# Causal attention and a routed second attention on one core: last queries of two head pairs in one set of 64x64 products, all scores in float32, tiles cleared ahead, a new order

## Chip, cores and metric

The kernel runs on one core of a Trainium2 chip. The metric is the device time of one launch in microseconds (us); lower is better. Engines: TensorE (PE in the profile, PEld its weight loads), VectorE (DVE), ScalarE (ACT), GpSimd (POOL), SyncE (SP), whose queue issues all DMAs here.

## What is computed

Batch 4, 12 heads of 64, 448 positions, all float32. First layer: causal softmax attention per head. Its output x (4, 448, 768) goes into a second layer with four experts, each a causal attention with one head of 64, whose outputs are weighted by a gate that keeps the two best of four experts:

```python
scores = np.where(mask, -1e9, 0.125 * q @ k.T)
attn = np.exp(scores - scores.max(-1)); attn /= attn.sum(-1) + 1e-9
x = heads_joined(attn @ v)
logits = x @ w_gate
for e in range(4):
    y[e] = causal_attention(x @ wq[e], x @ wk[e], x @ wv[e]) @ wo[e]
out = sum of w[token, e] * y[e] over the token's two experts
```

## The kernel before

**Work items.** The heads go in pairs: 24 pairs in the first layer (4 batches of 6) and 8 in the second (4 batches of 2 expert pairs). The 448 queries of a head are three blocks of 128 and a rest of 64. For a pair, `attention` (L384) lists these steps:

- Scores (L428 to L443). The two heads sit in the two halves of the 128 partitions, so a product contracts 64 rows, and the two heads' products (64x128 tiles) go to two PSUM banks. Block i meets only its first 128(i+1) keys. Blocks are made in two groups, block 1 and blocks 0 and 2.
- The last 64 queries of both heads (L447 to L454) are made in one product with 128 rows and 128 columns: the host writes these queries twice, each time with the other head's rows zero (L789), so that 128 contracted rows give head 0 in 64 output partitions and head 1 in the other 64. All 448 keys, one bank.
- Maximum on VectorE (L411), exponential on ScalarE (L417), reciprocal (L457), normalisation on GpSimd (L348; on ScalarE too in the second layer, L346).
- The weights are turned to have keys on partitions: for the pairs in `VIA` by two VectorE transposes (L485) and four SBUF-to-SBUF DMAs (L491), otherwise by 16 TensorE transposes in four banks (L500), each copied by ScalarE or VectorE.
- pv (L527): 128x64 tiles, the two heads side by side in the columns of the array. For each head and each of the two passes it streams 256+128+64 + 256+64 + 128+64 + 64 = 1,024 columns.
- The result is split into a high and a low part (L530 to L533) for the products that follow.

**Two number forms.** A float32 product is run as two passes. For the 17 first-layer pairs in `FULL` (L245) the scores are float32. For the other 7 pairs, and for all 8 of the second layer, queries and keys are split into a float32r high part (ScalarE, L554) and low part (GpSimd, L556; in the second layer VectorE, L600), and three float32r products (high-high, high-low, low-high) replace the float32 one (L422). In the second layer the doubled last queries are written by VectorE with a 0/1 mask `half` and split by GpSimd (L605 to L609).

**Second layer and output.** Queries and keys are projected from x (L579), values and gate logits (L635), the gate is ranked on VectorE (L668 to L696), and the output is projected (L714) and stored.

**What sets the order.** `Plan` (L54) holds all 1,514 steps with a cost per engine. `ORDER` (L248) is a written-out list of step numbers, found by a search outside the kernel; `run` (L93) walks it, gives each step to the engine that would end it first by the planned costs, gives it buffers from fixed counts (`HOMES`, L219: 9 `five` tiles for weights and their turned copies, 8 PSUM banks, 5 `raw`, 13 `two`), and emits it. Each engine then runs its instructions in that order. The plan starts all engines at 0, adds 0.2 us when TensorE changes between 128x128, 64x128 and 128x64 tiles (`SWITCH`, `TILING`), and knows nothing of a slow clock. When a `five` tile is first taken, two GpSimd memsets clear its padding (L240, L241): they stand in GpSimd's queue wherever the list happens to take the tile. GpSimd and VectorE share a port in the plan for some steps (`SHARED`).

**The start.** A VectorE memset and six TensorE products on it (L762), GpSimd's masks (L734, L736, L741 to L743 for `half`, L740 on VectorE), the loads on SP's queue, then pair 0, whose load comes in three parts.

Of the kernel before, what the change touches and what calls it, by code (L numbers as in the profile page):

```python
# [53 lines left out]
class Plan:  # L54
# [23 lines left out]
    def place(self, op, slots, make):  # L78
        taken = []
        for b in op.bufs:  # L80
            if b.at is None:
                home = make.home(b.kind)
                if len(slots[home]) < self.homes[home]:
                    slot = Slot(make(home))
# [45 lines left out]
def tile_attention_then_moe_attention(  # L130
# [52 lines left out]
    half = const.tile([P, 2], F32, name="half")  # L183
# [7 lines left out]

# [12 lines left out]
    def unit(h, i):  # L204
# [6 lines left out]
        "raw": ([P, W], F32), "two": ([P, W], F32R), "v": ([P, 2 * NC, HD], F32), "five": ([P, NG, SEG * G], F32),  # L211
        "stat": ([P, 3, NU], F32), "vb": ([P, NC, E, HD], F32), "gate": ([P, 2 + E, NC, E], F32),
        "rq": ([P, P], F32), "vs": ([P, VC], F32),
    }
    PS = ("s", "t", "acc", "pj", "big")
    RAW = ("raw", "w", "osb")
    TWO = ("hi", "lo", "bh", "bl", "x", "u")
    FIVE = ("p", "pt")
    HOMES = {"five": 9, "gate": 1, "ps": 8, "raw": 5, "rq": 1, "stat": 5, "two": 13, "v": 4, "vb": 1, "vs": 1}  # L219

    class Make:
        def __init__(self):
            self.n = defaultdict(int)

# [3 lines left out]
        def __call__(self, home):  # L228
            n = self.n[home]
            self.n[home] += 1  # L230
            if home == "ps" and n == 7:
                return last_bank
            if home == "ps":
                return psum.tile([P, 512], F32, tag=f"ps{n}", name=f"ps{n}")
            shape, dt = SHAPES[home]
            t = const.tile(shape, dt, tag=f"{home}{n}", name=f"{home}{n}")
# [147 lines left out]
    def attention(kind, b, p, ops, split_done, vals, v_ready, gate, dest):  # L384
# [16 lines left out]
        def spread(ap):  # L401
            return ap.rearrange("p (g t) -> p g t", g=NG)
# [410 lines left out]
```

## Time and profile before

| | us |
|---|---|
| median of 3 runs | 277.88 (277.48 to 278.42) |
| profiled execution | 277.25 |
| its span, first to last instruction | 275.4 |
| TensorE busy in the span | 264.5 (96%) |
| VectorE, ScalarE, GpSimd busy | 213.1, 182.9, 153.7 |
| mean granted TensorE clock | 0.994 of full |

Busy time of TensorE includes time in which a product waits in the array, and the ends of its products are modelled; how fast it works is read from the starts of successive products. A line of the profile such as L348 can be that of a helper that several steps use. The chain of waits follows the last instruction back to what released it. DMA moved 205 GB/s on average.

### The profile page before, as it was taken

Reading aid. Unit: us, or ns where it says so; the run is one execution under the profiler, and the core shown is the slowest. Engines: PE = TensorE matmul, PEld = TensorE weight load, DVE = VectorE, ACT = ScalarE, POOL = GpSimd, SP = SyncE. Lnnn points to the kernel's source line nnn. Section 1 sums busy time; section 2 is a strip of 40 time slices with the busy share of each in tenths; the row PEclk is TensorE's granted clock in tenths of the full one; section 3 lists DMA queues with packets and bytes.
Section 4 is the critical chain, followed back from the end, with each engine's and each line's share of the span. In section 5 each row is a group of like instructions: output and inputs, shape, how many; then the busy total and the mean of one; then the engine's idle time right before and its main releaser. Section 6 shows DMA issues by size and latency. Waiting matters only on the chain.

```text
span 275.4 us, 6959 instructions
## 1 busy us (share of the span) xinstructions
PE 264.5 (96%) x2349; PEld 223.3 (81%) x2349; DVE 213.1 (77%) x695; ACT 182.9 (66%) x601; POOL 153.7 (56%) x335
## 2 busy tenths in 40 slices
PE   8959799989999999999999999999999999999994
PEld 5537486878898878898988889899998899989884
DVE  2768898889978999899889799998988355595400
ACT  2839799967874369899747875869554514467223
POOL 6384958999675408968956977198440401043000
PEclk9979999999999999999999999999999999999999
DMA  6855668699688989697897969878888544008785
GB/s 214 298 166 176 221 144 291 143 287 284 180 235 237 250 218 329 148 245 224 219 259 207 257 182 211 240 167 233 223 224 215 159 95 126 1 0 227 183 296 200
DMA packets 27826, 56.55 MB, mean 205 GB/s; under 512 B 2960, under 2 KB 6416, under 8 KB 27792
## 3 DMA queue, kind: packets, MB, share of 16 engines
q1 hardware_dynamic: 27792, 56.12, 72.2%
q8 instruction: 18, 0.29, 0.4%
q14 instruction: 16, 0.13, 0.1%
HBM read 21.25 MB, written 5.51 MB: 97 GB/s over the span
## 4 chain that ended last, share of the span: by engine, by line
PE 75%; POOL 8%; ACT 5%; DVE 4%; DMA 3%; issue 3%; SPq 1%; POOLq 0%; DVEq 0%; ACTq 0%
PE ps L579 19%; PE ps L527 18%; PE ps L433 12%; PE ps L635 12%; PE ps L449 7%; POOL five L348 6%; PE ps L714 5%; ACT five L417 3%; DMA five<-five 3%; DVE five L485 1%; PE ps L500 1%; SPq L491 1%; DVE five L411 1%; PE ps L762 1%; ACT five L340 1%
## 5 line engine op out<-in xcount | busy, mean ns | idle before, releaser
L417 ACT ACTIVATE five<-five,stat 128x128 f32<-128x128 f32 (+3 forms) x224 | 116.2, 522 | 27.6 <-DVE stat L411 23.9
L348 POOL TENSOR_SCALAR five<-five,stat 128x256 f32<-128x256 f32 (+3 forms) x205 | 98.9, 503 | 31.5 <-DVE stat L457 28.3
L485 DVE STREAM_TRANSPOSE five<-five 128x1024 f32<-128x1024 f32 x56 | 67.5, 1226 | 6.7 <-POOL five L348 6.6
L579 PE MATMUL ps<-two,wqkh 128*128 128x448 f32 x192 | 56.3, 374 | 0.0
L411 DVE CUSTOM_DVE_ANT_1 five<-ps,mask 128x128 f32<-128x128 f32 (+1 forms) x128 | 42.5, 367 | 7.0 <-PE ps L433 5.4
L527 PEld LDWEIGHTS ps<-five,v 128*64 128x64 f32 x768 | 37.0, 137 | 11.5 <-issue 1.5
L527 PE MATMUL ps<-five,v 128*64 128x64 f32 (+2 forms) x768 | 45.5, 276 | 0.7 <-issue 0.7
L417 ACT ACTIVATION_READ_ACCUMULATOR five<-five,stat 128x1 f32 x224 | 42.5, 190 | 0.0
L340 ACT ACTIVATE two<-ps 128x448 fp32r<-128x448 f32 (+1 forms) x38 | 19.9, 528 | 29.7 <-PE ps L527 21.2
L579 PEld LDWEIGHTS ps<-two,wqkh 128*128 128x128 f32 x192 | 35.1, 188 | 4.2 <-issue 1.3
L352 DVE TENSOR_TENSOR two<-ps,two 128x448 fp32r<-128x448 f32 (+1 forms) x48 | 28.4, 603 | 11.5 <-ACT two L340 11.4
L411 DVE CUSTOM_DVE_ANT_0 five<-ps,mask 128x384 f32<-128x384 f32 x64 | 36.3, 587 | 1.2 <-PE ps L433 1.2
L579 PE MATMUL ps<-two,wqkl 128*128 128x448 f32 x96 | 34.9, 364 | 0.0
L635 PE MATMUL ps<-wvh,two 128*128 128x260 f32 x168 | 33.3, 288 | 0.0
L635 PEld LDWEIGHTS ps<-wvh,two 128*128 128x128 f32 x168 | 27.5, 188 | 1.4 <-issue 0.7
L433 PE MATMUL ps<-raw 64*128 64x384 f32 (+2 forms) x204 | 28.3, 408 | 0.0
L714 PE MATMUL ps<-two,woh 128*128 128x448 f32 x96 | 27.7, 370 | 0.0
L635 PE MATMUL ps<-wvl,two 128*128 128x260 f32 x96 | 26.2, 282 | 0.0
L411 DVE CUSTOM_DVE_ANT_0 five<-ps,maskr 128x448 f32<-128x448 f32 x32 | 20.8, 661 | 4.8 <-POOL five L241 2.3
L433 PEld LDWEIGHTS ps<-raw 64*128 64x128 f32 x204 | 17.8, 194 | 7.6 <-issue 1.2
L411 DVE DVE_READ_ACCUMULATOR2_ANT stat<- 128x1 f32 x224 | 20.9, 93 | 0.0
L714 PEld LDWEIGHTS ps<-two,woh 128*128 128x128 f32 x96 | 17.8, 188 | 1.8
(88 smaller groups left out, 359.2 us busy)
## 6 DMA issues: line engine op xcount, KB each, us to landing
five<-five SPq DMA_DIRECT2D x112, 256.0 KB, 4.7
raw<-in_qk_dram SPq DMA_DIRECT2D x23, 480.0 KB, 5.6
v<-in_v_dram SPq DMA_DIRECT2D x24, 256.0 KB, 5.0
out_dram<-raw SPq DMA_DIRECT2D x9, 448.0 KB, 4.7
raw<-in_wqk_dram SPq DMA_DIRECT2D x4, 384.0 KB, 4.1
out_dram<-raw SPq DMA_DIRECT2D x6, 224.0 KB, 2.0
raw<-in_wvg_dram SPq DMA_DIRECT2D x2, 390.0 KB, 5.7
raw<-in_wo_dram SPq DMA_DIRECT2D x2, 384.0 KB, 5.2
```

The source lines that it names most:

```text
L340: nc.scalar.activation(out, in_, AF.Copy)
L348: (nc.gpsimd if e == "POOL" else nc.vector).tensor_scalar(t, t, r, 1.0, op0=ALU.mult, op1=ALU.mult)
L352: eng.tensor_tensor(out=out, in0=a, in1=b, op=ALU.subtract)
L411: lambda e: nc.vector.tensor_tensor_reduce(out=by_key(w(h, i)), in0=spread(src.at[:, at:at + wide(i)]), in1=mk, scale=-0.125, scalar=3.0e3 ...
L417: lambda e: nc.scalar.activation(w(h, i), w(h, i), AF.Exp, bias=stat.at[:, 0, u:u + 1], scale=-1.0, accum_out=stat.at[:, 1, u:u + 1],), [m ...
L433: nc.tensor.matmul(spread(banks[h].at[:, at[i]:at[i] + m]), ops[x].at[sides[h], QUE + i * P:QUE + m], spread(ops[y].at[sides[h], KEY])[:, ...
L449: nc.tensor.matmul(tail.at[:, :S], ops[x].at[:, REM:W], ops[y].at[:, KEY], start=(n == 0), stop=(n == len(terms) - 1),)
L485: add(("tr", me), "tr", {"DVE": T_TURN}, lambda e, g=g: nc.vector.transpose(pb.at[:, g:g + 2].rearrange("p g k -> p (g k)"), pb.at[:, g:g ...
L527: nc.tensor.matmul(o, vals(h, j), t, start=(n == 0), stop=(n == len(parts) - 1), skip_group_check=True)
L579: nc.tensor.matmul(ps.at[:, :S], w[:, 2 * sel + p, k], halves(xbuf[b, k].at, t), start=(k == 0 and n == 0), stop=(k == NP - 1 and n == 2),)
L635: nc.tensor.matmul(ps.at[:, :VC], xbuf[b, k].at[:, at + c * P:at + c * P + P], w[:, k], start=(k == 0 and n == 0), stop=(k == NP - 1 and n ...
L714: nc.tensor.matmul(ps.at[:, :S], w[:, p, m * P:m * P + P], halves(ubuf[b, p].at, t), start=(p == 0 and n == 0), stop=(p == 1 and n == 2),)
```

## The change

1. The host no longer doubles the last queries: `qk` is 448 keys and 448 queries. The last 64 queries of two pairs are scored together (`quarters`, kind `sq`): two products per pair, each 64 rows by 64 columns, so that pair 0's two heads and pair 1's two heads take the four quarters of the array; one bank per pair, head 0 in its lower and head 1 in its upper partitions for the first pair, the other way round for the second (`swap`). In the first layer pairs are listed by twos (`couple`), and the step waits for both loads; in the second layer for both expert pairs.
2. All scores are float32. `FULL`, the splits of the first layer, the low parts and doubled last queries of the second layer and `half` are gone. Blocks 0 to 2 are scored in 64x64 tiles: two halves of the queries for each of two heads.
3. All tiles are made when the plan starts, and VectorE clears their padding there, ahead of every planned step.
4. The last pair of the second layer, (3, 1), leaves `VIA`: TensorE turns it.
5. The plan starts its engines at given times (`BEGIN`), lengthens TensorE's steps before 6.9 us (`COLD`), has a few other costs, other buffer counts (`raw` 8, `two` 8 for x and u alone, `v` 6, `vb` 2), and `ORDER` is searched anew (1,439 steps).

The core of the diff (the list, some costs and the lines that only follow from these are left out):

```diff
     ENGINES = ("PE", "ACT", "DVE", "POOL", "DMA")
+    BEGIN = {"PE": 0.0, "ACT": 2.1, "DVE": 4.5, "POOL": 4.0, "DMA": 0.8, "port": 4.5}
+    COLD = 6.9
     FROM_PE, FROM_REST, FROM_DMA, SWITCH = 0.22, 0.2, 0.1, 0.2
     LANDING = 2.0
-    TILING = defaultdict(int, s=1, pv=2)
-    SHARED = ("hi", "lo", "w", "norm")
+    TILING = defaultdict(int, s=1, pv=2, sq=1)
+    SHARED = ("w", "norm")
...
     def run(self, order, make):
-        free = {e: 0.0 for e in [*self.ENGINES, "port"]}
+        free = dict(self.BEGIN)
         slots = defaultdict(list)
-        copied, last = 0.8, None
+        copied, last = self.BEGIN["DMA"], None
+        self.tiles = {home: make.tiles(home, count) for home, count in self.homes.items()}
...
                 if e == "PE" and last and self.TILING[last.kind] != self.TILING[op.kind]:
                     d += self.SWITCH
+                if e == "PE":
+                    d += max(0.0, min(d, (self.COLD - start) / 2))
...
-    RAW = ("raw", "w", "osb")
-    TWO = ("hi", "lo", "bh", "bl", "x", "u")
+    RAW = ("raw", "w", "osb", "bq")
+    TWO = ("x", "u")
     FIVE = ("p", "pt")
-    HOMES = {"five": 9, "gate": 1, "ps": 8, "raw": 5, "rq": 1, "stat": 5, "two": 13, "v": 4, "vb": 1, "vs": 1}
+    HOMES = {"five": 9, "gate": 1, "ps": 8, "raw": 8, "stat": 5, "two": 8, "v": 6, "vb": 2, "vs": 1}
...
-            if home == "vb":
-                nc.gpsimd.memset(t[R:, NF], 0.0)
-            if home == "five":
-                nc.gpsimd.memset(t[:, :, SEG * G - G // 2:], 0.0)
-                nc.gpsimd.memset(t[:, NG - 1, SEG * G - R:], 0.0)
-            return t
+            made = [const.tile(shape, dt, tag=f"{home}{n}", name=f"{home}{n}") for n in range(count)]
+            for t in made if home == "vb" else ():
+                nc.vector.memset(t[R:, NF], 0.0)
+            for t in made if home == "five" else ():
+                nc.vector.memset(t[:, :, SEG * G - G // 2:], 0.0)
+                nc.vector.memset(t[:, NG - 1, SEG * G - R:], 0.0)
+            return made
...
-    FULL = (0, 1, 2, 3, 4, 5, 6, 7, 8, 9, 11, 12, 13, 14, 15, 19, 20)
...
-    T_SCORE = (0.25, 0.36, 0.55, 0.61)
-    T_FULL = (0.24, 0.46, 0.70, 0.82)
+    T_SCORE = (0.24, 0.46, 0.70)
+    T_QUAD = 0.83
...
-        terms = ((0, 0), (0, 1), (1, 0))[:2 * len(ops) - 1]
-        cost = T_SCORE if len(ops) == 2 else T_FULL
         for group in ((1,), (0,), (2,)) if (kind, b, p) == ("a", *pairs[0]) else GROUPS:
             banks = [Buf("s"), Buf("s")]
             at = {i: sum(k + 1 for k in group if k < i) * P for i in group}
 
             def mm(e, group=group, at=at, banks=banks):
-                for n, (x, y) in enumerate(terms):
-                    for i in group[::-1]:
-                        m = (i + 1) * P
-                        for h in range(2):
-                            nc.tensor.matmul(
-                                spread(banks[h].at[:, at[i]:at[i] + m]), ops[x].at[sides[h], QUE + i * P:QUE + m],
-                                spread(ops[y].at[sides[h], KEY])[:, :, :m // NG],
-                                start=(n == 0 and i == group[-1]), stop=(n == len(terms) - 1 and i == group[0]),
-                                skip_group_check=True,
-                            )
-
-            s = add(("s%d" % len(group), me), "s", {"PE": sum(cost[i] for i in group)}, mm, split_done[:4] if max(group) < 2 else split_done, banks + ops)
+                for i in group[::-1]:
+                    m = (i + 1) * P
+                    for c, h in ((0, 0), (1, 1), (1, 0), (0, 1)):
+                        q = QUE + i * P + c * HD
+                        nc.tensor.matmul(
+                            spread(banks[h].at[sides[c], at[i]:at[i] + m]), oper.at[sides[h], q:q + HD],
+                            spread(oper.at[sides[h], KEY])[:, :, :m // NG],
+                            start=(i == group[-1]), stop=(i == group[0]), skip_group_check=True,
+                        )
+
+            s = add(("s%d" % len(group), me), "s", {"PE": sum(T_SCORE[i] for i in group)}, mm, ready[:4] if max(group) < 2 else ready, banks + [oper])
             for i in group:
                 for h in range(2):
                     softmax(s, banks[h], at[i], h, i)
 
-        tail = Buf("s")
-
-        def last(e):
-            for n, (x, y) in enumerate(terms):
-                nc.tensor.matmul(
-                    tail.at[:, :S], ops[x].at[:, REM:W], ops[y].at[:, KEY], start=(n == 0), stop=(n == len(terms) - 1),
-                )
-
-        s = add(("sr", me), "sr", {"PE": cost[NF]}, last, split_done, [tail] + ops)
+        s, tail = rest
         softmax(s, tail, 0, 0, NF)
...
-                        t = pt.at[:, 2 * h:2 * h + 2, seg(h, NF, j) * G:seg(h, NF, j) * G + G]
+                        t = pt.at[:, 2 * (h ^ swap):2 * (h ^ swap) + 2, seg(h, NF, j) * G:seg(h, NF, j) * G + G]
...
-        if not full:
-            hi = add(("hi", me), "hi", {"ACT": 0.91}, lambda e: copy(e, hb.at, raw.at), ready, [raw, hb])
-            ready = [hi] + [
-                add(("lo", me), "lo", {"POOL": 1.18}, lambda e, at=at: sub(e, lb.at[:, at], raw.at[:, at], f32(hb.at)[:, at]), [hi], [raw, hb, lb])
-                for at in (slice(0, W // 2), slice(W // 2, W))
-            ]
...
+    def quarters(me, ops, ready):
+
+        tails = [Buf("s"), Buf("s")]
+
+        def last(e):
+            for n, t in enumerate(ops):
+                for h in range(2):
+                    nc.tensor.matmul(
+                        tails[n].at[sides[h ^ n], :S], t.at[sides[h], REM:REM + R], t.at[sides[h], KEY], start=True, stop=True,
+                    )
+
+        return add(("sq", me), "sq", {"PE": T_QUAD}, last, ready, tails + ops), tails
+
+    def couple(b, p):
+        members = [first_layer(b, p), first_layer(b, p + 1)]
+        s, tails = quarters((b * NP + p) // 2, [m[0] for m in members], members[0][1] + members[1][1])
+        for tail, (_, _, softmaxes) in zip(tails, members):
+            softmaxes((s, tail))
...
-        opsb = [[Buf("bh"), Buf("bl")] for _ in range(2)]
+        opsb = [Buf("bq"), Buf("bq")]
...
-                h_ = add(("hb", 4 * b + 2 * p + sel), "hb", {"ACT": 0.43, "DVE": 0.65},
-                         lambda e, o=o, ps=ps, put=put, got=got: copy(e, put(o[0]), got(ps)), [prev], [ps] + o)
-                l_ = add(("lb", 4 * b + 2 * p + sel), "lb", {"DVE": 0.54},
-                         lambda e, o=o, ps=ps, put=put, got=got: sub(
-                             e, put(o[1]), got(ps), f32(put(o[0]))), [h_], [ps] + o)
-                ready[p] += [h_, l_]
-                if not sel:
-                    rq = Buf("rq")
-                    d = add(("rq", 2 * b + p), "rq", {"DVE": 0.25}, lambda e, ps=ps, rq=rq: nc.vector.tensor_tensor(
-                        out=rq.at.rearrange("p (h r) -> p h r", h=2), in0=ps.at[:, NF * P:S].unsqueeze(1).to_broadcast([P, 2, R]),
-                        in1=half.unsqueeze(2).to_broadcast([P, 2, R]), op=ALU.mult), [prev], [ps, rq])
-                    h_ = add(("rq", 2 * b + p), "hr", {"POOL": 0.37}, lambda e, o=o, rq=rq: copy(e, o[0].at[:, REM:W], rq.at), [d], [rq] + o)
-                    l_ = add(("rq", 2 * b + p), "lr", {"POOL": 0.43}, lambda e, o=o, rq=rq: sub(
-                        e, o[1].at[:, REM:W], rq.at, f32(o[0].at)[:, REM:W]), [h_], [rq] + o)
-                    ready[p] += [h_, l_]
+
+                def put(e, o=o, ps=ps, sel=sel):
+                    if sel:
+                        copy(e, spread(o.at[:, KEY]), ps.at[:, :S].rearrange("p (t g) -> p g t", g=NG))
+                    else:
+                        copy(e, o.at[:, QUE:QUE + S], ps.at[:, :S])
+
+                ready[p].append(add(("hb", 4 * b + 2 * p + sel), "hb", {"ACT": 0.43, "DVE": 0.65}, put, [prev], [ps, o]))
...
+        s, tails = quarters(B * NP // 2 + b, opsb, ready[0] + ready[1])
...
-    for b, p in pairs:
-        first_layer(b, p)
+    for b, p in pairs[::2]:
+        couple(b, p)
...
-        "qk": np.concatenate([kt, qt[..., :NF * P], last.reshape(B, H // 2, 2 * D, 2 * R)], axis=3),
+        "qk": np.concatenate([kt, qt], axis=3),
```

## Rows read from the trace of the kernel before

**Rows 1.** The page: busy us (share of the span) and instructions of each engine.

```profile
PE 264.5 (96%) x2349; PEld 223.3 (81%) x2349; DVE 213.1 (77%) x695; ACT 182.9 (66%) x601; POOL 153.7 (56%) x335
```

**Rows 2.** Windows: stretch, length; busy PE, PEld, DVE, ACT, POOL; granted clock; DMA.

```profile
13.70:17.60 3.90, 0.72 (x5) 0.42 (x4) 1.20 (x5) 0.06 (x1) 3.73 (x11) 0.98 0.60 193
17.60:21.00 3.40, 3.29 (x10) 2.25 (x10) 3.40 (x15) 2.53 (x7) 2.49 (x2) 0.52 0.42 120
21.00:48.00 27.00, 25.15 (x246) 17.90 (x244) 23.43 (x93) 24.99 (x89) 19.30 (x44) 1.00 0.69 211
60.00:160.00 100.00, 100.00 (x926) 86.04 (x921) 89.87 (x309) 74.75 (x252) 71.34 (x135) 1.00 0.85 235
160.00:272.00 112.00, 111.48 (x999) 99.42 (x997) 77.95 (x227) 62.18 (x196) 38.53 (x93) 1.00 0.65 176
```

**Rows 3.** Chain of waits in order of time: start, us, engine, line, instructions.

```profile
17.71 1.86 PE ps L449 x2
...
36.85 3.63 ACT five L417 x14
...
49.90 0.44 PE ps L500 x4
...
61.80 1.50 PE ps L449 x4
...
66.81 1.92 PE ps L527 x32
...
73.16 0.60 PE ps L449 x3
...
229.29 1.36 PE ps L433 x18
```

**Rows 4.** Line L449, from 48 us to the end: min/median/max ns, first and last start.

```profile
L449 PE MATMUL ps<-raw x16: 537/539/643, 50.2 to 137.5; 128*128 128x448 f32 x16
L449 PE MATMUL ps<-two x15: 361/367/472, 73.0 to 248.1; 128*128 128x448 f32 x15
```

**Rows 5.** Timeline of TensorE around a score run of one float32 pair.

```profile
42.41 1.57 PE L433 MATMUL ps<-raw 64*128 64x384 f32 x12
43.91 0.65 PE L527 MATMUL ps<-five,v 128*64 128x256 f32 x4
```

**Rows 6.** Timeline: weight loads of the last pv.

```profile
263.57 1.88 PEld L527 LDWEIGHTS ps<-five,vb 128*64 128x64 f32 x32 [0.71 <-issue]
```

**Rows 7.** Groups by form, split steps: count | busy us, mean ns | idle before.

```profile
L352 DVE TENSOR_TENSOR two<-ps,two 128x448 fp32r<-128x448 f32 x40 | 24.1, 614 | 11.5 <-ACT two L340 11.4
L352 POOL TENSOR_TENSOR two<-raw,two 128x480 fp32r<-128x480 f32 x14 | 17.0, 1229 | 2.5 <-issue 1.7 <-ACT two L340 0.8
L340 ACT ACTIVATE two<-raw 128x960 fp32r<-128x960 f32 x7 | 7.0, 996 | 0.8 <-DMA raw<-in_qk_dram 0.8
L352 DVE TENSOR_TENSOR two<-ps,two 128x384 fp32r<-128x384 f32 x8 | 4.4, 547 | 0.0
```

**Rows 8.** Timeline of the start: clears, and who waits for them.

```profile
3.11 0.20 DVE L740 COPY maskr<-maskr 64x64 f32<-64x64 f32 x1 [2.06 <-POOL half L741]
...
4.81 0.39 DVE L411 CUSTOM_DVE_ANT_1 five<-ps,mask 128x128 f32<-128x128 f32 x1 [1.50 <-PE ps L433]
...
14.44 0.15 POOL L240 MEMSET five<- 128x64 f32 x1
...
14.82 0.62 DVE L411 CUSTOM_DVE_ANT_0 five<-ps,maskr 128x448 f32<-128x448 f32 x1 [2.33 <-POOL five L241]
...
17.03 0.62 DVE L411 CUSTOM_DVE_ANT_1 five<-ps,mask 128x256 f32<-128x256 f32 x1 [1.57 <-POOL five L240]
...
17.54 0.60 ACT L340 ACTIVATE five<-ps 128x512 f32<-128x512 f32 x1 [4.20 <-POOL five L241]
```

**Rows 9.** Timeline of the start: pair 1's first scores, first normalisation.

```profile
8.72 2.00 PE L433 MATMUL ps<-raw 64*128 64x384 f32 x16
...
11.48 3.01 POOL L348 TENSOR_SCALAR five<-five,stat 128x256 f32<-128x256 f32 x6 [5.95 <-DVE stat L457]
```

More of the change, by code (lines that the diff above doesn't have):

```diff
@@ L83, in place @@
                 if len(slots[home]) < self.homes[home]:
-                    slot = Slot(make(home))
+                    slot = Slot(self.tiles[home][len(slots[home])])
                     slots[home].append(slot)
@@ L217, in tile_attention_then_moe_attention, with tiles @@
-    TWO = ("hi", "lo", "bh", "bl", "x", "u")
+    RAW = ("raw", "w", "osb", "bq")
+    TWO = ("x", "u")
     FIVE = ("p", "pt")
-    HOMES = {"five": 9, "gate": 1, "ps": 8, "raw": 5, "rq": 1, "stat": 5, "two": 13, "v": 4, "vb": 1, "vs": 1}
+    HOMES = {"five": 9, "gate": 1, "ps": 8, "raw": 8, "stat": 5, "two": 8, "v": 6, "vb": 2, "vs": 1}
     class Make:
-        def __init__(self):
-            self.n = defaultdict(int)
         def home(self, kind):
             return "ps" if kind in PS else "raw" if kind in RAW else "two" if kind in TWO else "five" if kind in FIVE else kind
[L228 to L232, printed above, removed]
+        def tiles(self, home, count):
@@ L233, in __call__ @@
             if home == "ps":
-                return psum.tile([P, 512], F32, tag=f"ps{n}", name=f"ps{n}")
+                return [last_bank if n == 7 else psum.tile([P, 512], F32, tag=f"ps{n}", name=f"ps{n}") for n in range(count)]
             shape, dt = SHAPES[home]
-            t = const.tile(shape, dt, tag=f"{home}{n}", name=f"{home}{n}")
-            if home == "vb":
-                nc.gpsimd.memset(t[R:, NF], 0.0)
-            if home == "five":
-                nc.gpsimd.memset(t[:, :, SEG * G - G // 2:], 0.0)
-                nc.gpsimd.memset(t[:, NG - 1, SEG * G - R:], 0.0)
@@ L246, in tile_attention_then_moe_attention @@
-    VIA = [("a", *pairs[n]) for n in [2, 4, 6, 7, 8, 9, 10, 11, 12, 13, 14, 15, 16, 17, 18, 19, 20, 21, 22, 23]] + [("b", b, p) for b, p in [(0, 0), (0, 1), (1, 0), (1, 1), (2, 0), (2, 1), (3, 0), (3, 1)]]
+    VIA = [("a", *pairs[n]) for n in [2, 4, 6, 7, 8, 9, 10, 11, 12, 13, 14, 15, 16, 17, 18, 19, 20, 21, 22, 23]] + [("b", b, p) for b, p in [(0, 0), (0, 1), (1, 0), (1, 1), (2, 0), (2, 1), (3, 0)]]
     GROUPS = ((1,), (0, 2))
     ORDER = (
[74 rows of a table removed]
[70 rows of a table added]
     )
@@ L542, in first_layer @@
         me = b * NP + p
-        raw, vt, hb, lb = Buf("raw"), Buf("v"), Buf("hi"), Buf("lo")
-        first = (b, p) == pairs[0]
-        full = b * NP + p in FULL
+        raw, vt = Buf("raw"), Buf("v")
         ready = []
-        if first:
-            for at in (KEY, slice(QUE, QUE + 2 * P), slice(QUE + 2 * P, W)):
-                ready.append(add(("ld", me), "ld", {"DMA": (0.45, 0.1 + (at.stop - at.start) / 1200, 3.0)}, lambda e, at=at: nc.sync.dma_start(raw.at[:, at], qk[b, p, :, at]), (), [raw]))
+        if me == 0:
+            for at in (KEY, slice(QUE, QUE + 2 * P), slice(QUE + 2 * P, 2 * S)):
+                ready.append(add(("ld", me), "ld", {"DMA": (0.45, 0.6 if at.stop == 2 * S else 0.15, 3.0)}, lambda e, at=at: nc.sync.dma_start(raw.at[:, at], qk[b, p, :, at]), (), [raw]))
@@ new lines, in softmaxes @@
+        def softmaxes(rest):
+            dest = xbuf[b, p] = Buf("x")
+            xdone[b, p], xrest[b, p] = attention(
+                "a", b, p, raw, ready, lambda h, j: vt.at[:, h * NC + j], [vl, vt], None, dest, rest
+            )
+        return raw, ready, softmaxes
+    def quarters(me, ops, ready):
[5 more added lines that the diff above has]
+                        tails[n].at[sides[h ^ n], :S], t.at[sides[h], REM:REM + R], t.at[sides[h], KEY], start=True, stop=True,
+                    )
+        return add(("sq", me), "sq", {"PE": T_QUAD}, last, ready, tails + ops), tails
@@ L740, in masks @@
         nc.vector.tensor_copy(maskr[R:, :, -G // 2:], maskr[:R, :, -G // 2:])
-        nc.gpsimd.memset(half, 0.0)
-        for h in range(2):
-            nc.gpsimd.memset(half[sides[h], h:h + 1], 1.0)
     def lowers(e):
@@ L788 @@
     kt = heads_t(k).reshape(B, H // 2, 2 * D, S // 4, 4).swapaxes(3, 4).reshape(B, H // 2, 2 * D, S)
-    last = np.zeros((B, H // 2, 2, D, 2, R), q.dtype)
-    for h in range(2):
-        last[:, :, h, :, h] = qt[:, :, h * D:(h + 1) * D, NF * P:]
     vp = np.zeros((B, H // 2, 2, NC * P, D), v.dtype)
```

35 lines of the change are left out of this document (12 added, 23 removed), and 144 rows, old and new, of the table ORDER.

## The prediction

> **What bounds the kernel now.** I read the page first [rows 1]: TensorE is busy 96% of the span, VectorE 77%, ScalarE 66%, GpSimd 56%. An average over stages hides two regimes, so the windows come next [rows 2]. From 60 to 272 us TensorE is busy all but 0.5 us. Before 48 us it is not the limit: from 13.7 to 17.6 us GpSimd works almost alone (3.73 of 3.90 us; VectorE 1.20, ScalarE 0.06, TensorE 0.72), and from 21 to 48 us ScalarE is busy 24.99 of 27 us. The chain of waits says the same [rows 3]: softmax pieces such as the 3.63 us of ScalarE at 36.85 carry it up to 48 us, TensorE pieces after that. So work taken off TensorE after about 48 us shortens the kernel one for one; before 48 us it is worth nothing by itself, and only what starts the softmax engines sooner counts.
>
> **The change, part by part.** The sum is made against the profiled execution (277.25 us, span 275.4); the median of the runs shown, 277.88, is 0.6 us above it, and I carry the difference over to it.
>
> *Last queries.* Today each pair has one 128x128 product over zero-padded queries. In float32 (17 pairs) it is two passes of 0.375 us: two products are x4 in 1.50 us [rows 3]. Split in three float32r terms (15 pairs: 7 of the first layer, 8 of the second) it takes 0.60 us [rows 3]. After 48 us there are 16 float32 passes, so 8 such products, and all 15 split ones [rows 4]: 8 x 0.75 + 15 x 0.60 = 15.0 us. The new form makes one "sq" for two pairs: four 64x64 tiles, each with two passes of 448 columns. No row shows four tiles at once. Two row tiles side by side do overlap fully: a score run of one float32 pair streams 2 x (128+256+384) columns per head, which at 0.375 us per 448 is 1.286 us for one head alone, and the run of both heads takes 43.91 - 42.41 = 1.50 us to the start of the next product [rows 5]. Two column tiles overlap too: pv has 2 heads x 2 passes x 1,024 columns, 3.43 us one after another, and takes 1.92 [rows 3]. Bounds for sq: 0.75 us if all four stream together, 1.50 us if only two do. Both kinds of overlap are measured, so I stay near the lower end and take 0.85, a tenth more for starting two further tiles. About 11 of 16 sq fall after 48 us (9 of the 24 first-layer products lie before it now): 11 x 0.85 = 9.35. **Gain 5.65 us.** The Trainium skill, "TensorE: Matmul & The Clock Gate", Part 3 (Packing small matmuls), says that tiles in different places of the array start about 4 ns apart and that the span is that of one product plus 4 ns per further tile; by it an sq would be about 0.76 us, an estimate, and the kernel 1 us faster than I say. No run here shows four tiles yet.
>
> *Scores of the first 384 queries.* Pairs already in float32 keep their columns: twice as many products of half the height, four abreast, where the 1.50 us run had two. Lower bound the same time, upper bound twice (a rival below). The 15 split pairs go from three float32r terms (x18 in 1.36 us [rows 3]) to float32 (1.50 [rows 5]): 15 x 0.14 = 2.1; the 1.36 leaves out some of the switch that the 1.50 holds, so I take a **loss of 1.8 us**, all after 53 us.
>
> *The last pair is turned by TensorE* instead of VectorE and four DMAs on SP's queue: 4 x 0.44 us of transposes [rows 3] are added, and the stall of 0.71 us ahead of the last pv [rows 6] can go, since nothing waits for those transfers any more. Four copies from PSUM replace two VectorE transposes, beside TensorE's output projection. **Loss 1.0 us** (from 0 to 1.8).
>
> *Tile switches.* The 1.50 us run has about 0.2 us over its 1.286 us of columns: about what changing the array's tiling costs. The old products lie among 128x128 work for nothing. An sq next to a score group costs no switch more; alone it costs two, so 0 to 11 x 0.4 = 4.4 us. A list can place it next to one, so I take 0.
>
> *Splits.* Gone are, by count and mean [rows 7]: 14 GpSimd subtractions of 1.23 us, 7 ScalarE copies of 1.00, on VectorE 8 of 0.614 and 8 of 0.547 (9.3 us), and the small steps of the doubled queries. I cost them at nothing after 48 us: TensorE covers them, and VectorE, at 90% from 60 to 160 us [rows 2], gets 9 us lighter while TensorE gets about 3 us lighter, so no other engine becomes the bound. If that cover were gone, VectorE would be late next.
>
> *Clearing moved from GpSimd's queue to VectorE, ahead of everything.* Nine tiles are cleared twice each, at 0.15 us [rows 8]. The memsets stand in GpSimd's queue behind normalisations, and at 14.8 and 17.0 us VectorE has waited 2.33 and 1.57 us for them, at 17.5 us ScalarE 4.20 us [rows 8]. TensorE comes out of that hole, 0.72 us busy in 3.90, with a granted clock of 0.52 of full speed, the 1.2 GHz level for nearly all of 17.6 to 21.0 us [rows 2], and two passes take 1.86 us instead of 0.75 [rows 3]. Best case: the 3.9 us hole closes and 1.1 us of slow clock with it, 5.0 us. Price: 18 clears of about 0.15 (the nearest memset is GpSimd's [rows 8]) and two larger ones are 3 us on VectorE, which is idle from 3.31 to 4.81 us [rows 8], so its first maximum starts up to 1.5 us later, and ScalarE's first exponential behind it. A second wait: a pair's last scores now wait for the next pair's load too. Pair 1's first scores run at 8.72 us [rows 9]; an sq behind them ends at about 9.6, which leaves 1.9 us for a maximum, an exponential and a reciprocal until GpSimd's first normalisation at 11.48 [rows 9]: 0 to 1 us late, with GpSimd's queue of normalisations behind it. SP's loads get 7% smaller. Between +1 and -5 us I take **a gain of 2.5 us**, half of the best case: ScalarE is nearly saturated right behind the hole and holds back the rest.
>
> Sum: -5.65 + 1.8 + 1.0 - 2.5 = -5.35 us, so 271.9 for the profiled execution and **272.5 us** for the median.
>
> **The rivals.**
> 1. *The start gives nothing*: VectorE's late first maximum and ScalarE's load eat the closed hole. For it: ScalarE 24.99 of 27 us [rows 2]. Against it: ScalarE and VectorE both stood still in the hole. Time: 277.88 - 2.85 = 275.0. Chance 0.17.
> 2. *No change*: most sq stand alone between other tilings (+4.4 us). Against it: score groups come all through the kernel. 277.88 - 5.35 + 4.4 = 276.9, about 0.3% (0.8 us) under the time before, which is what a measurement of this kernel can tell from no change. Chance 0.07.
> 3. *Slower, by the bank*: in an sq both row halves of the array write into one PSUM bank (other partitions of it), which no product of the kernel before does: the two heads of a score group go to two banks, and the two column tiles of pv share their rows. If that serialises them, an sq costs 1.50: 11 x 0.65 = 7.2 us more, so 279.7. It decides from about 1.35 us per sq on. The Trainium skill, "TensorEngine Tiling (Array Packing)", Restrictions and Gotchas, says that different row tiles cannot access the same PSUM bank at once; by that rule this is what would happen, and no row of this trace shows it or excludes it. Chance 0.09.
> 4. *The change does not do what it says*: four tiles never run more than two abreast, in score groups too. 23 pairs after 48 us (8 float32 and 15 split, as many as last-query products) would each cost 1.29 us more, and the sq 7.2: about 309 us. Against it: pv already gets 32 products through in 1.92 us, 0.06 us each [rows 3], and here a pass streams 128 columns or more. Chance 0.05.
>
> **How the numbers follow.** The forecast has 0.62: 0.62 + 0.17 = 0.79 faster, 0.07 same, 0.09 + 0.05 = 0.14 slower. The low end takes the whole hole (2.5 us more), sq at 0.75 (1.1) and part of the turning for nothing (0.4): 268.5. The high end takes in rivals 1 and 2 with 0.4 us for the size of the terms: 277.3. Rivals 3 and 4 (0.14) and a little at both ends are left out.
>
> **What would show it.** Right: 128 matmuls on the sq line, in fours, a pass about 0.375 us; float32 score runs of one pair still about 1.5 us; no 128x128 last scores, no split subtractions of queries and keys; no clearing by GpSimd and no wait for one; TensorE saturated from about 45 us instead of 48, without the half clock at 17 us. Wrong: an sq of 1.1 us or more, score runs near 2.8 us, switches around every sq, TensorE idle after 60 us, or a hole at the start that has merely moved.

## The result and the profile after

The changed kernel takes **270.03 us** (269.10 to 270.84, 4 runs) against 277.68 beside it: ratio 0.9721 [0.9682, 0.9759], 7.65 us less, where 5.35 less was forecast. Its profiled execution is 269.91 us, the span 268.2, the mean granted clock 1.000. Ratios are against the kernel before, run beside each kernel, and of fast runs alone; one run here is not, e3's at 274.63 us, 2.5% above that kernel's fastest. The page's busy line, beside [rows 1]:

```profile
PE 256.8 (96%) x2708; PEld 204.4 (76%) x2708; DVE 202.1 (75%) x685; ACT 176.2 (66%) x585; POOL 134.5 (50%) x300
```

The windows of after (stretch, length; busy PE, PEld, DVE, ACT, POOL; granted clock; DMA). The second to fourth and the last answer to [rows 2]:

```profile
0.00:13.70 13.70, 11.35 (x105) 6.58 (x108) 9.84 (x50) 7.59 (x25) 6.07 (x26) 1.00 0.82 310
13.70:17.60 3.90, 3.90 (x39) 2.25 (x35) 3.90 (x24) 3.87 (x16) 2.69 (x6) 1.00 0.59 204
17.60:21.00 3.40, 3.23 (x39) 2.56 (x35) 3.40 (x13) 3.40 (x12) 3.23 (x8) 1.00 0.46 111
21.00:48.00 27.00, 25.50 (x332) 18.66 (x334) 23.19 (x87) 24.62 (x84) 22.12 (x35) 1.00 0.77 228
13.70:48.00 34.30, 32.63 (x403) 23.46 (x401) 30.49 (x118) 31.89 (x109) 28.05 (x47) 1.00 0.72 214
48.00:264.00 216.00, 212.19 (x2214) 174.07 (x2205) 161.75 (x519) 136.20 (x452) 100.36 (x228) 1.00 0.72 197
60.00:160.00 100.00, 96.71 (x1095) 76.52 (x1088) 86.07 (x290) 67.87 (x240) 55.01 (x120) 1.00 0.83 224
```

The hole at 14 to 17 us is gone: all four engines work there, and the granted clock at 17.6 to 21.0 us is 1.00 where it was 0.52 [rows 2]. But from 60 to 160 us TensorE, busy all of it before, now stands still for 3.3 us. Three longer stretches of before, to set beside these:

```profile
0.00:13.70 13.70, 12.60 (x62) 7.80 (x62) 7.32 (x29) 7.69 (x23) 6.60 (x33) 1.00 0.74 256
13.70:48.00 34.30, 29.16 (x259) 20.56 (x258) 28.03 (x109) 27.59 (x95) 25.52 (x56) 0.95 0.65 200
48.00:264.00 216.00, 214.87 (x1971) 188.10 (x1973) 177.10 (x557) 143.79 (x477) 121.54 (x248) 1.00 0.74 202
```

Length less PE busy is TensorE's idle time. Before to after it goes 1.1 to 2.4 us up to 13.7 us, 5.1 to 1.7 up to 48 us, and 1.1 to 3.8 from 48 to 264 us. Over the span it is 10.9 before and 11.4 after. So the gain stands wholly in TensorE's busy time (264.5 to 256.8), and idle time that left the start came back elsewhere. That balance hides two effects, which the experiments separate.

The new last-query step, by its line and on TensorE's timeline, beside [rows 4, 5]:

```profile
L551 PE MATMUL ps<-raw x128: 536/536/587, 6.9 to 225.1; 64*64 64x448 f32 x128
```

```profile
59.84 0.93 PE L551 MATMUL ps<-raw 64*64 64x448 f32 x8
60.59 0.61 PE L425 MATMUL ps<-raw 64*64 64x256 f32 x8
```

Eight products (four tiles, two passes) start at 59.84 and the next work at 60.59: 0.75 us per sq. A product's own 536 ns is longer than the 375 ns after which the next four start, so products overlap. The chain of waits after, beside [rows 3]:

```profile
57.27 2.75 PE ps L425 x48
...
110.75 1.46 PE ps L425 x24
...
182.94 5.00 DMA five<-five
...
198.74 1.64 SPq L474
...
206.00 4.23 DMA five<-five
210.36 1.99 PE ps L510 x32
...
249.16 1.75 PE ps L483 x16
```

A score run is x24 in 1.46 us (1.50 before), two in a row take 2.75, and turning the last pair is x16 in 1.75. Transfers of weights being turned (L474, `five<-five`) stand in the chain between 29 and 210 us; in the chain of before they stand only from 246 us on:

```profile
247.44 4.19 DMA five<-five
...
258.69 4.78 DMA five<-five
```

The pv at 210.36 follows the end of such a transfer at 210.23. All the starts of pv (L510) after 48 us that TensorE waited for, with the wait in brackets:

```profile
93.80 1.99 PE L510 MATMUL ps<-five,v 128*64 128x256 f32 x32 [1.74 <-DVE gate L674]
...
141.92 1.99 PE L510 MATMUL ps<-five,v 128*64 128x256 f32 x32 [0.93 <-DVE stat L440]
...
157.67 1.99 PE L510 MATMUL ps<-five,v 128*64 128x256 f32 x32 [0.63 <-ACT two L332]
...
210.36 1.99 PE L510 MATMUL ps<-five,v 128*64 128x256 f32 x32 [0.51 <-DMA five<-five]
```

They sum to 3.81 us, all of the idle time of the 48 to 264 window. The names of the first three releasers mislead: in the trace's DMA records the last turned weights of these pairs land at 93.67, 141.72 and 157.53 us, 0.13 to 0.2 us ahead of each start, as at 210.23. All four pv wait for a transfer.

### The profile page after: what moved, and what is told of

Same layout as the page of the kernel before. It is cut to its first block, busy times and chain, and to the rows that moved or that the text cites. A ratio compares the mean times of both kernels' runs of the same rounds, so it can differ in the third digit from the quotient of the medians.

```text
span 268.2 us, 7602 instructions
## 1 busy us (share of the span) xinstructions
PE 256.8 (96%) x2708; PEld 204.4 (76%) x2708; DVE 202.1 (75%) x685; ACT 176.2 (66%) x585; POOL 134.5 (50%) x300
## 4 chain that ended last, share of the span: by engine, by line
PE 67%; DVE 12%; SPq 8%; DMA 5%; ACT 3%; issue 2%; POOL 1%; POOLq 0%; DVEq 0%
PE ps L577 18%; PE ps L510 15%; PE ps L696 11%; PE ps L425 10%; PE ps L617 9%; SPq L474 8%; DVE five L405 7%; DMA five<-five 5%; PE ps L551 3%; DVE five L468 3%; ACT five L411 1%; PE ps L483 1%; ACT five L332 1%; SPq L534 1%; ACT two L332 0%
## 5 line engine op out<-in xcount | busy, mean ns | idle before, releaser
L411 ACT ACTIVATE five<-five,stat 128x384 f32<-128x384 f32 (+3 forms) x224 | 116.1, 522 | 23.0 <-DVE stat L405 19.8
L340 POOL TENSOR_SCALAR five<-five,stat 128x128 f32<-128x128 f32 (+3 forms) x207 | 100.1, 509 | 40.5 <-DVE stat L440 19.1
L468 DVE STREAM_TRANSPOSE five<-five 128x1024 f32<-128x1024 f32 x54 | 65.3, 1227 | 8.9 <-POOL five L340 8.6
L405 DVE CUSTOM_DVE_ANT_1 five<-ps,mask 128x256 f32<-128x256 f32 (+1 forms) x128 | 43.9, 372 | 12.9 <-PE ps L425 10.8
L425 PE MATMUL ps<-raw 64*64 64x384 f32 (+2 forms) x768 | 51.4, 387 | 1.2 <-DMA raw<-in_qk_dram 0.9
L510 PE MATMUL ps<-five,v 128*64 128x64 f32 (+2 forms) x768 | 46.1, 276 | 4.8 <-DVE gate L674 1.7
L510 PEld LDWEIGHTS ps<-five,v 128*64 128x64 f32 x768 | 37.6, 137 | 15.6 <-issue 2.2
L425 PEld LDWEIGHTS ps<-raw 64*64 64x64 f32 x768 | 27.3, 134 | 24.4 <-issue 14.6
L405 DVE CUSTOM_DVE_ANT_0 five<-ps,mask 128x384 f32<-128x384 f32 x64 | 37.0, 597 | 1.6 <-PE ps L425 1.6
L332 ACT ACTIVATE raw<-ps 128x448 f32<-128x448 f32 x28 | 15.1, 541 | 22.7 <-PE ps L577 11.3
L332 ACT ACTIVATE two<-ps 128x448 fp32r<-128x448 f32 x27 | 14.6, 541 | 20.6 <-PE ps L510 20.5
L344 DVE TENSOR_TENSOR two<-ps,two 128x448 fp32r<-128x448 f32 x32 | 19.5, 613 | 10.5 <-ACT two L332 10.3
```

What stands on the lines that cost most here:

```text
L332: nc.scalar.activation(out, in_, AF.Copy)
L340: (nc.gpsimd if e == "POOL" else nc.vector).tensor_scalar(t, t, r, 1.0, op0=ALU.mult, op1=ALU.mult)
L344: eng.tensor_tensor(out=out, in0=a, in1=b, op=ALU.subtract)
L405: lambda e: nc.vector.tensor_tensor_reduce(out=by_key(w(h, i)), in0=spread(src.at[:, at:at + wide(i)]), in1=mk, scale=-0.125, scalar=3.0e3 ...
L411: lambda e: nc.scalar.activation(w(h, i), w(h, i), AF.Exp, bias=stat.at[:, 0, u:u + 1], scale=-1.0, accum_out=stat.at[:, 1, u:u + 1],), [m ...
L425: nc.tensor.matmul(spread(banks[h].at[sides[c], at[i]:at[i] + m]), oper.at[sides[h], q:q + HD], spread(oper.at[sides[h], KEY])[:, :, :m // ...
```

## Experiments

### The clears alone, on the old kernel

**e4**: the kernel before, with its list, scores and splits; only the clears move ahead of everything, onto VectorE. **e5**, run later: the same on GpSimd, whose first normalisation comes at 11.48 us [rows 9]; **e10** repeats e5 beside the changed kernel (**e9**).

```diff
-                    slot = Slot(make(home))
+                    slot = Slot(self.tiles[home][len(slots[home])])
...
+        self.tiles = {home: [make(home) for _ in range(count)] for home, count in self.homes.items()}
...
-                nc.gpsimd.memset(t[:, :, SEG * G - G // 2:], 0.0)
+                nc.vector.memset(t[:, :, SEG * G - G // 2:], 0.0)
```

(The last two lines and the two other memsets are e4's only.)

> The kernel before with one part of the change alone: all tiles made at the start and cleared by VectorE there, old list. My theory: the 3.9 us in which everything waits for GpSimd's clears close, half of it and of the slow clock comes through: 2.5 us less than before, about 275.2 (274 to 276.5). Rival (ScalarE's load and the later first maximum take it back, and the list decides): within 0.8 us of 277.7.

> The kernel before, all tiles made at the start and cleared there, but by GpSimd, old list. The run with VectorE's clears alone gave about 5.6 us. My theory: what counts is that the clears leave GpSimd's queue of normalisations, not which engine makes them; GpSimd has nothing to normalise before 11.5 us, so the same gain: 271.5 to 273. Rival (VectorE is the better place; GpSimd's 18 clears and a larger one, 3 us, delay the masks' followers and the first maximum, which waits for the first clear): half of it, 274 to 276.

Measured: e4 271.87 us, ratio 0.9792 [0.9737, 0.9846]; e5 270.33, 0.9729 [0.9690, 0.9768]. The clears alone are worth 5.6 us on VectorE and, on GpSimd, as much as the whole change. e5's page and windows:

```profile
PE 263.6 (98%) x2349; PEld 222.5 (83%) x2349; DVE 212.5 (79%) x695; ACT 182.9 (68%) x601; POOL 154.3 (57%) x335
```

```profile
0.00:13.70 13.70, 12.59 (x63) 8.01 (x64) 8.23 (x32) 7.69 (x23) 8.63 (x48) 1.00 0.76 253
13.70:17.60 3.90, 3.90 (x29) 2.69 (x29) 3.90 (x17) 3.73 (x13) 3.82 (x7) 1.00 0.65 207
21.00:48.00 27.00, 26.60 (x229) 19.58 (x228) 25.15 (x89) 26.67 (x97) 22.95 (x44) 1.00 0.76 220
13.70:48.00 34.30, 33.90 (x300) 24.94 (x300) 32.38 (x122) 33.77 (x120) 30.09 (x53) 1.00 0.77 229
48.00:264.00 216.00, 215.55 (x1986) 188.44 (x1984) 171.87 (x543) 140.08 (x458) 115.58 (x237) 1.00 0.74 205
```

The span falls from 275.4 to 269.0: idle time of TensorE from 10.9 to 5.4, of which 4.7 at 13.7 to 48 us, and 0.9 of busy time, which the half clock at 17.6 to 21.0 us can account for. ScalarE, 24.99 of 27 us at 21 to 48 us before [rows 2], now reaches 26.67: it was not full. Of the 2.01 us in which it stood still before, 1.80 are a wait for one more clear, the one that GpSimd made at 30.56 us, and TensorE waited 1.51 us for what ScalarE did next:

```profile
30.75 1.09 ACT L340 ACTIVATE five<-ps 128x512 f32<-128x512 f32 x2 [1.80 <-POOL five L241]
...
31.39 0.66 PE L500 MATMUL ps<-ident,five 128*128 128x128 f32 x4 [1.51 <-ACT five L340]
```

Taken product by product (e5 has the same list), TensorE in e5 is 4.4 us ahead at the transposes that start at 19.36 us before, 6.7 at those that start at 31.39, and 6.4 at the last product. So the gain is made by 31 us.

e4's median lies 1.5 us above e5's. The intervals overlap and the chips differ, but none of e4's 4 runs (271.60 to 272.01) reaches down to the 10 of e5 and e10 (269.98 to 271.17). VectorE's clears do hold up the first maximum, e4's timeline first, then e5's:

```profile
3.91 0.11 DVE L241 MEMSET five<- 128x64 f32 x1
...
6.20 0.39 DVE L412 CUSTOM_DVE_ANT_1 five<-ps,mask 128x128 f32<-128x128 f32 x1
```

```profile
4.82 0.38 DVE L412 CUSTOM_DVE_ANT_1 five<-ps,mask 128x128 f32<-128x128 f32 x1 [1.49 <-PE ps L434]
```

VectorE's clears hold it up by 1.4 us; GpSimd's cost it nothing (4.81 before [rows 8]). But this is not where the 1.5 us come from: at the transposes that start at 41.28 us in e5, e4 is only 0.16 us behind. It falls back at one pv, whose turned weights land late, e4 first:

```profile
51.32 3.75 PE L528 MATMUL ps<-five,v 128*64 128x256 f32 x64 [1.99 <-DMA five<-five]
```

```profile
49.92 3.75 PE L528 MATMUL ps<-five,v 128*64 128x256 f32 x64 [0.36 <-issue]
```

In the trace the third of that pair's four transfers took 2.41 us to be issued in e4 and 0.60 in e5; the last landed at 51.23 and 49.83 us. Whether VectorE's clears have a part in that is open.

### Changed kernel and clears alone, side by side, and a third clear

**e11** is the changed kernel with its clears up front on GpSimd (the memsets' `nc.vector` becomes `nc.gpsimd`), its list as it was.

> The changed kernel again, beside the next run on the same chip, because the kernel before with its clears moved alone came as low as the whole change. My theory now: the whole gain of the change is the clears; the rest (sq, float32, list) gives TensorE about 7 us less work and gets nothing for it: 270.0, within 0.8 us of the next run. Rival (the rest is worth the 2 to 3 us that the prediction gave it): 2 to 3 us under the next run.

> The kernel before with its clears made by GpSimd ahead of everything, again, beside the run above. My theory now: 270.3, the same as the whole change. Rival: 272 to 273.

> The changed kernel, list untouched, with the clears ahead of everything on GpSimd instead of VectorE. In the kernel before GpSimd was 1.5 us better than VectorE in this place, since VectorE's first maximum came 1.4 us earlier. My theory: softmax engines pace the start, so 0.5 to 1.5 us less than the changed kernel: 268.5 to 269.5. Rival (the list was made for VectorE's later start; transfers set TensorE's waits later): no change within 0.8 us.

Measured, 6 runs each: e9 270.34 us, 0.9738 [0.9695, 0.9782]; e10 270.51, 0.9756 [0.9722, 0.9790]; e11 269.21, 0.9703 [0.9661, 0.9744]. e9 and e10 can't be told apart, but they differ in the engine of their clears too (VectorE and GpSimd). Their windows, e9 first:

```profile
13.70:48.00 34.30, 32.66 (x403) 23.51 (x401) 30.55 (x118) 31.92 (x109) 28.04 (x47) 1.00 0.72 217
48.00:264.00 216.00, 211.97 (x2210) 174.29 (x2203) 161.72 (x519) 135.76 (x452) 100.42 (x228) 1.00 0.72 196
```

```profile
13.70:48.00 34.30, 34.00 (x305) 25.38 (x305) 32.32 (x121) 34.17 (x123) 30.59 (x53) 1.00 0.77 230
48.00:264.00 216.00, 214.44 (x1976) 187.49 (x1972) 171.74 (x541) 139.03 (x454) 114.93 (x236) 1.00 0.73 204
```

The changed kernel has 6.5 us less TensorE work (256.3 against 262.8 by their pages) and, with spans of 268.7 and 269.3 us, 5.9 us more idle time: 1.3 at 13.7 to 48 us, 2.5 from 48 to 264 us, and 2.1 before 13.7 us. With the clears on the same engine on both sides, the changed kernel stays ahead a little: e11 is 1.3 us under e10, with 7.4 us less TensorE work (255.4 against 262.8), and the changed kernel 1.8 under e4, with 6.4 less (256.8 against 263.2). The intervals overlap in both comparisons, so the rest of the change is worth some 1 to 2 us in these runs, not clear of noise. e11 lies 1.1 us under e9 with overlapping intervals: it suggests that VectorE was the dearer place here too, and does not show it.

### The last queries two abreast

**e1**: both pairs of an sq use the same two quarters of the array; everything else is as in the changed kernel.

```diff
-        swap = p % 2
+        swap = 0
...
-                        tails[n].at[sides[h ^ n], :S], t.at[sides[h], REM:REM + R], t.at[sides[h], KEY], start=True, stop=True,
+                        tails[n].at[sides[h], :S], t.at[sides[h], REM:REM + R], t.at[sides[h], KEY], start=True, stop=True,
```

> The changed kernel, but the last queries of both pairs of an sq use the same two quarters of the array (no swap of the second pair's heads), so that only two of the four products can run side by side. My theory: an sq takes 1.50 us instead of 0.75, and about 12 of the 16 lie after the start, where TensorE is the bound one for one: 12 x 0.75 = 9 us more, about 279 us. Rival (TensorE has idle time between 60 and 160 us in the changed kernel, 3.3 us, which would swallow part): 4 to 6 us more, 274 to 276. Second rival (the four products never were abreast): no change, 270.

Measured: 274.75 us (273.92 to 275.34), 0.9895 [0.9836, 0.9953], 4.7 more than after. Its page, window and chain:

```profile
PE 266.2 (97%) x2708; PEld 208.4 (76%) x2708; DVE 202.4 (74%) x685; ACT 176.4 (65%) x585; POOL 133.9 (49%) x300
```

```profile
48.00:264.00 216.00, 215.24 (x2203) 172.59 (x2200) 162.96 (x523) 133.55 (x447) 99.93 (x228) 1.00 0.71 194
```

```profile
148.29 1.49 PE ps L551 x8
```

An sq is 1.49 us, twice 0.75, so four abreast is real. TensorE gets 9.4 us busier, yet the kernel only 4.7 us longer: its idle time from 48 to 264 us falls from 3.8 to 0.8, and only two pv still wait there, which fits transfers that catch up with a slower TensorE. In this list a microsecond of TensorE is worth about half.

### Scores in 64x128 tiles

**e2**: blocks 0 to 2 in the old 64x128 tiles, float32 as in the changed kernel.

```diff
-                    for c, h in ((0, 0), (1, 1), (1, 0), (0, 1)):
-                        q = QUE + i * P + c * HD
+                    for h in range(2):
+                        q = QUE + i * P
```

> The changed kernel, but blocks 0 to 2 of the queries are scored in 64x128 tiles as before, in float32, half as many products of twice the height; sq and the list stay. My theory: the columns and so the time of a score run are the same (about 1.28 us per pair), and only the switches of the tiling next to each sq come on top: 12 sq after the start with one or two switches of about 0.2 us, 2.4 to 4.8 us more, 272.5 to 275. Rival (twice as many products and weight loads cost TensorE time): a pair's run gets shorter and the whole is at or under 270.

Measured: 271.92 us (270.80 to 272.21), 0.9785 [0.9716, 0.9854], 1.9 more than after, with overlapping intervals; TensorE busy 260.4 us, 3.6 more. Smaller tiles with the same columns are no dearer, and here cheaper. The trace shows where, at the sq that is shown above for after:

```profile
57.10 2.87 PE L425 MATMUL ps<-raw 64*128 64x256 f32 x24
59.89 0.98 PE L551 MATMUL ps<-raw 64*64 64x448 f32 x8
60.81 0.70 PE L425 MATMUL ps<-raw 64*128 64x256 f32 x4
```

These scores and their sq take 4.34 us up to the next projection (57.10 to 61.44), and 3.93 in after (57.20 to 61.13): 0.2 us for each of the two borders between sq and scores, where the array's tiling changes here and not in after. Away from an sq a pair's score run takes 1.50 us here and 1.46 in after. So most of the difference stands at these borders.

### Clears back in GpSimd's queue

**e3**: the changed kernel with each tile cleared by GpSimd when it is first taken, as before.

```diff
                     slots[home].append(slot)
+                    make.clear(home, slot.tile)
```

> The changed kernel, but a tile is cleared by GpSimd at the place in its queue where the list first takes the tile, as before. My theory: the hole at the start opens again in part, VectorE and ScalarE wait for a clear behind normalisations: 1.5 to 4 us more, 271.5 to 274. Rival (the new list and its truer start times made the start shorter, the clears do not matter): within 0.8 us of 270.

Measured: 270.73 us, but 267.96 to 274.63; ratio 0.9719 [0.9631, 0.9806], where after has 0.9721. No loss can be seen, nor one of 2 us be excluded. TensorE is busy 32.90 of 34.30 us at 13.7 to 48 us, so there is no hole. The clears still stand among GpSimd's normalisations, the last at 26.07 us (32.03 before), but the longest waits that the trace puts down to one are 0.41 and 0.17 us, of TensorE's weight loads. The place in the queue is a hazard of one list, not a price of GpSimd.

### The last pair by transfers again

**e6**: pair (3, 1) goes back into `VIA`; VectorE and four DMAs turn it, at their places in the list.

```diff
-VIA = [... (2, 0), (2, 1), (3, 0)]]
+VIA = [... (2, 0), (2, 1), (3, 0), (3, 1)]]
```

> The changed kernel, but the last pair of the second layer is turned by VectorE and four DMAs again; its two transposes and four transfers stand where the last of its TensorE transposes stood, the rest of the list is the same. My theory: 1.75 us of TensorE work go, but the last pv then waits for transfers of about 5 us with only the last output products to fill in: 1 to 4 us slower, 271 to 274. Rival (TensorE is bound to the end, as the prediction had it): up to 1 us faster, 269 to 270.

Measured: 275.18 us (273.40 to 276.34), 0.9897 [0.9837, 0.9956], 5.1 more than after. TensorE's waits ahead of the last two pv (`vb`):

```profile
251.40 1.99 PE L500 MATMUL ps<-five,vb 128*64 128x256 f32 x32 [1.06 <-DMA five<-five]
...
257.04 3.34 PE L500 MATMUL ps<-five,vb 128*64 128x256 f32 x32 [3.65 <-DMA five<-five]
```

4.7 us of waits stand where 1.75 us of transposes stood. After the longer wait the granted clock is down to 0.57 of full speed, the 1.2 GHz level for most of this stretch, and the last pv takes 3.34 us where the one ahead of it takes 1.99:

```profile
257.00:261.00 4.00, 3.96 (x34) 3.44 (x35) 0.01 (x1) 0.55 (x1) 0.00 (x0) 0.57 1.03 380
```

This is the fastest of the four runs, 273.40 us. Before, the same place cost 0.71 us [rows 6]. That the transfers go as they did, and the work that covered them is gone, is my reading; it was not tried.

### Other lists

**e7**: the changed kernel in the old order, as far as the steps of old and new correspond. **e8**: the changed kernel with another new list.

> The changed kernel with the list of before: steps that both have keep the old order, an sq stands where the second of its two last-query products stood, and a step that cannot go yet (its pair's sq or a buffer is missing) follows as soon as it can. My theory: coupling two pairs holds PSUM banks and weight tiles, so the old order stalls: over 280 us; the gain needs a list made for the coupling. Rival (the list is worth little, the steps themselves make the gain): 270 to 274.

> The changed kernel, steps untouched, with another list, which keeps TensorE from the idle time it has between 60 and 200 us. My theory: that run with two products abreast showed idle time of TensorE (11 us in all) that the list can still use: 1 to 2 us less, 268 to 269. Rival (the changed kernel's idle time is set by VectorE and by the chain at the start): no change within 0.8 us.

Measured: e7 301.48 us (2 runs), 1.0848 [1.0767, 1.0930]; TensorE busy 91% of its span. The new steps lose in the old order. That an sq, which needs both pairs' loads and two banks at once, holds up what stands behind it is my reading and not shown: TensorE waits 1.5 us in all ahead of sq, and its longest waits are 5.6 us ahead of a pv and 4.8 ahead of a transpose. e8 273.49 us, 0.9849 [0.9804, 0.9895], a miss of its theory. Its largest wait at pv (us in total, times, longest), in its fastest run of 271.94 us:

```profile
PE ps L500 <- DVE gate L664: 3.6, 1, 3.6
```

One pv alone waits 3.6 us; here too the turned weights landed 1 to 5 us after the time that the kernel's plan gives them.

### A version that beats both

**e12**: the changed kernel with clears on GpSimd up front, start times for the plan that follow from that, 1.5 us more for the landing of turned weights in the plan, and a list searched with these.

```diff
-    BEGIN = {"PE": 0.0, "ACT": 2.1, "DVE": 4.5, "POOL": 4.0, "DMA": 0.8, "port": 4.5}
+    BEGIN = {"PE": 0.0, "ACT": 2.1, "DVE": 3.4, "POOL": 7.6, "DMA": 0.8, "port": 4.5}
...
-                end = copied + self.LANDING
+                end = copied + self.LANDING + (1.5 if op.kind == "mv" else 0.0)
```

> The changed kernel with the clears on GpSimd ahead of everything and a list made for planned transfers of the turned weights that land 1.5 us later, as the trace of the changed kernel shows them to land against its plan, so that pv does not wait for them. My theory: the four waits ahead of pv after 48 us (3.8 us in all) shrink to under 1 us, and the start gains up to 1: 265.5 to 268. Rival (any list finds its waits elsewhere, as the second list did): 269 to 272.

Measured: **266.61 us** (265.94 to 267.77, 6 runs), 0.9618 [0.9578, 0.9657], 3.7 under the changed kernel beside it. Its windows, then its waits at pv:

```profile
13.70:48.00 34.30, 34.30 (x432) 24.43 (x432) 33.71 (x129) 34.02 (x124) 31.74 (x60) 1.00 0.77 245
48.00:264.00 216.00, 209.79 (x2168) 174.09 (x2164) 155.33 (x497) 136.38 (x446) 91.08 (x204) 1.00 0.72 196
```

```profile
91.09 1.99 PE L500 MATMUL ps<-five,v 128*64 128x256 f32 x32 [2.46 <-DMA five<-five]
...
156.03 1.99 PE L500 MATMUL ps<-five,v 128*64 128x256 f32 x32 [0.42 <-DMA v<-in_v_dram]
...
200.27 1.99 PE L500 MATMUL ps<-five,vb 128*64 128x256 f32 x32 [0.74 <-POOL stat L438]
```

The gain comes from the start: TensorE is busy every moment from 13.7 to 48 us, and VectorE and ScalarE nearly so; up to 48 us it is idle 1.9 us, against 4.8 in e9. (The second window takes in part of the kernel's end, which came 3.7 us sooner: 3.7 of its 6.2 idle us lie before 260.3 us.) The part of the theory about transfers missed: 3.6 us of waits at pv are left of 3.8. Its three edits (engine of the clears, plan, list) were not tried apart.

## Why the prediction was right, and where its sum was not

The sign and the range held. The sum was 2.3 us short, and that it came so near is in part luck: the clears gave about 3 us more than was taken, the rest of the change about 1 less.

- **Clears, -2.5 us: mis-sized.** Alone they are worth 5.6 us (e4), or 7 to 8 on an idle engine (e5, e10). The step that failed is "ScalarE is nearly saturated right behind the hole and holds back the rest", and with it the best case of 5.0 us: of the 2.01 us that ScalarE was not busy there, 1.80 were a wait for a further clear, at 30.75 us, which the best case left out. TensorE lost 1.85 us behind the hole (25.15 of 27 [rows 2]), of which 1.45 came back too (26.60 in e5). The first maximum late by up to 1.5 us was right, 1.4 in e4, but at 41 us it had cost TensorE only 0.16.
- **Last queries, cost right, worth wrong.** 0.85 us was taken; 0.75 was measured beside score work, the lower bound, and up to 0.88 elsewhere. Ten sq fall after 48 us, not 11, and take 8.03 us in all where 9.35 was taken. Rivals 3 and 4 fall with it and with score runs of 1.46. By the Trainium skill, "TensorE: Matmul & The Clock Gate", Part 3 (Packing small matmuls), an sq would be about 0.76 (an estimate); the measurement agrees, though the tiles start some 7 ns apart and not 4. The bank rule of the Trainium skill, "TensorEngine Tiling (Array Packing)", Restrictions and Gotchas, does not hold for these products: both row halves write one bank, on different partitions, at the full rate. What failed is "work taken off TensorE after about 48 us shortens the kernel one for one". In e1, 9.4 us of it were worth 4.7. With the clears on the same engine, 6.4 us less (after and e4) and 7.4 less (e11 and e10) were worth 1.8 and 1.3, where these terms were given 2.85. One of the prediction's own signs of being wrong came: TensorE idle after 60 us.
- **No other engine becomes the bound: true of engines, but not of transfers.** I asked whether VectorE would be late next and did not ask it of the DMAs that turn the weights, though the chain of before held them too (at 247.44 and 258.69 us). They are late at four pv, 3.81 us in all. That they land just ahead of each start is shown; e8's list and e12's, the second planned with later landings, did not cure it, so how to is open.
- **Before 48 us TensorE's work is worth nothing by itself: borne out.** By 48 us the trace has the same work done in the changed kernel, e4 and e5 (128 pv products, 64 transposes, 18 projection products), although the first one's TensorE was idle 2.5 us longer. Before, it was 128, 48 and 6.
- **Float32 scores, +1.8.** A run is 1.46 us where 1.50 was taken, against 1.36 for the split form: 15 x 0.10 = 1.5. The split form was not tried in 64x64 tiles.
- **Turning the last pair, +1.0: wrong sign in this list.** Undoing it costs 5.1 us (e6). The transposes' 1.75 us were right; the stall they remove is 4.7 us here and brings a slow clock, where 0.71 was counted.
- **Tile switches, 0: nearly.** Five of the ten sq after 48 us stand between score work with nothing added, 0.75 us from start to next as at 59.84; the other five take 0.80 to 0.88, 0.5 us more in all.
- **Rival 1** (the start gives nothing) falls by e4 and e5; **rival 2** by the number.

Open: what e3's new list does that GpSimd's clears don't hurt it (its spread, 3.7 us even without the 274.63, hides 2 us), and which of e12's edits carries its gain. No run gives the old steps, with their clears moved, a list searched anew, so how much of the 1 to 2 us beyond the clears is the steps and how much the list is open too.

## What to carry to other kernels

Read what a queue holds ahead of an engine's first needs: memsets of 0.15 us, put wherever a buffer is first taken, cost 6 to 8 us here through two engines and the clock, and moving them needed none of the rest of the change. Before counting work off an engine that is 96% busy one for one, ask what each of its steps will be waiting for once it arrives sooner, transfers included. Where a total agrees with a sum of several terms, run each large term by itself: here the range held, and a term taken at 2.5 us measured 5.6.

## What the runs showed of the hardware that was not expected

- Four 64x64 float32 products in the four quarters of the array start 20 ns apart in all (about 7 ns each), and the next four follow 375 ns later: four streams of 448 columns in the time of one, with row halves sharing a PSUM bank.
- A 256 KB transfer inside SBUF took 4.8 us (median) from issue to landing in after, 3.5 to 6.3, at a DMA share of 0.72 from 48 to 264 us; its issue on SP's queue took up to 1.64 us (chain at 198.74).
- The same small clear takes 0.11 us on VectorE and 0.15 on GpSimd (e4 and e5).
- After a wait of 3.65 us TensorE's granted clock was 0.57 from 257 to 261 us in e6, and a pv took 3.34 us instead of 1.99.
